# A fused short convolution and two-layer GELU network: which blocks use seven products instead of eight, with new instruction lists for four engines

## The chip, the cores and the metric

The kernel runs on one core of a Trainium2 chip. A core has TensorE (PE in the profile, with its weight loads as PEld), VectorE (DVE), ScalarE (ACT), GpSimd (POOL) and SyncE (SP), which run separate instruction queues and wait for one another by semaphores, and 16 DMA engines that serve transfers issued by SyncE, ScalarE and GpSimd. The metric is the device time of one execution in microseconds, less is better.

## The reference

```python
# x: 8 x 4096 x 192 (batch, sequence, features), 8 heads of 24 features, 7 taps
w = softmax(weight)                                   # 8 x 7, per head
out = sum over k of w[head, k] * x_padded[:, s + k]   # causal, zeros before the sequence
h = out.reshape(32768, 192) @ w_in                    # 192 x 2048
g = 0.5 * h * (1 + erf(h / sqrt(2)))                  # exact GELU
return g @ w_out                                      # 2048 x 192, float32
```

## The kernel before, in words

The 32768 tokens lie in two halves of 16384 that are worked on together, the one on partitions 0 to 63, the other on 64 to 127 (64 of the 192 features at a time). The tokens of each half are cut into 35 blocks (`NB`): blocks 0 to 5 have 256 tokens, blocks 6 to 34 have 512. What follows is about the blocks of 512.

For a block n, VectorE transposes the input (`t` n, line 1023) and adds up the seven taps of the convolution in float32 (line 359; the steps `1` to `6` of its lists); the zeroth tap is ScalarE's (`f0.n` to `f2.n`, line 1157). The sixth step writes `xc`, of which there are five buffers (`NXC`). TensorE multiplies `xc` by `w_in` (`mm1`, line 1292, 192 matmuls a block on quarter tiles of 64 x 64, four of which run side by side: 48 rounds); ScalarE applies GELU (line 1199, 16 instructions a block) and writes `gT` in bf16, of which there are two buffers. While TensorE is in block n with `mm1`, it also multiplies `gT` of block n-1 by `w_out`, in portions between the portions of `mm1`. There are two ways of doing this:

- In a plain block (`mm2_t`, line 1377) that is 192 matmuls, 48 rounds. Three transposes of VectorE (`ev.0`, `ev.1`, `ev.2`, line 477) bring the result from PSUM to the output buffer `osb`.
- In a seven-product block (those in `ST`; `mm2_s`, line 1426) some of the two-by-two products are formed the way Strassen and Winograd do, with seven products where eight stood: 44 rounds. This takes sums of parts of `gT`: `S1` (line 734, three parts), `S3` (737; parts 0 and 1 by accumulating DMAs of GpSimd, line 691, part 2 by VectorE), `Dn` (740, two parts) and `S4` (743, two parts). Behind the products come copies from PSUM by ScalarE (`p15`, `e`, `u`, `p3`, line 782), DMAs of GpSimd that copy `u` to the other partitions (`cu`, `cg`, line 686), combinations by VectorE (`k0`, line 790; `k3`, 797; `k4`, 803) and three transposes (line 815). Part 0 of `Dn` is VectorE's if the block before is a seven-product block too; otherwise it is made by two DMAs of GpSimd (`cp`, line 717, and `Dn.0`, line 721).

PSUM gives 2 x 2 banks to `mm1` (`hp`) and four to the second multiplication (`ob`); which of the four a block may use is worked out in advance (`BK`, `REL`), and TensorE waits for the step that frees a bank: `ev.2`, `k4`, `u`, `p3` or `e` of a seven-product block, the `ev` of a plain one.

The order on each engine is written out by hand. `LIST[n]` holds VectorE's steps while it prepares block n, as in `t19 ev.0.14 1 S1.0.16 2 ...` (name, part, block). `SLOT[n]` holds ScalarE's steps ahead of the i-th GELU of block n (`5:f2.20`). `GLIST` is GpSimd's order, with the copies of the last six tokens to the next block (`halo.n`, line 931). `AHEAD[n]` says up to which block SyncE has loaded before it stores block n-1 (`store`, line 845; four DMAs, one for each quarter of the partitions). The steps `w.0` to `w.9` make sums of the weights `w_out`, `evac` (line 438) brings the result of block 5 to `osb`. Block 34 ends the kernel: its products (line 1482) on whole tiles, four groups g of 128 tokens with two halves h, then `evac_half` (449 by VectorE, 451 by ScalarE) and `store_half` (459). The first group waits for the GELUs four by four:

```python
if (g, h) == (0, 0) and i % 4 == 0:
    t.wait_ge(S_GELU, SL0[m] + i + 4)
```

Of the kernel before, what the change touches and what calls it, by code (L numbers as in the profile page):

```python
# [11 lines left out]
def bass_lightweight_conv__then__act_gelu_exact_kernel(  # L12
# [41 lines left out]
    AHEAD = {4: 11, 5: 11, 7: 13, 8: 15, 9: 16, 10: 16, 11: 19, 12: 19, 13: 20, 14: 21, 15: 22, 16: 23, 17: 25, 18: 25, 19: 25, 22: 26, 23: 31, 24: 31, 25: 33, 26: 33, 27: 33, 28: 35, 29: 35}  # L54
# [20 lines left out]
    ST = [m for m in [8, 10, 11, 13, 14, 16, 17, 19, 20, 22, 24, 25, 27, 29, 30, 31, 32, 33] if m < M1]  # L75
    TYPE = {m: "S" if m in ST else "N" for m in range(-4, NB + 4)}
    LIST = {
        4: "t5 w.0.0 w.1.0 1 2 w.2.0 3 4 5 6",
        5: "t6 1 2 3 4 w.3.0 5 6",
        6: "w.4.0 t7 1 w.5.0 2 w.6.0 3 4 5 6",  # L80
        7: "t8 1 2 3 evac.0.5 w.7.0 4 5 6",
        8: "evac.1.5 t9 1 2 3 4 5 6",
        9: "ev.0.6 1 t10 2 ev.2.6 3 ev.1.6 4 5 w.8.0 6",
        10: "t11 1 2 S1.0.8 3 S1.1.8 ev.0.7 w.9.0 4 ev.1.7 S1.2.8 ev.2.7 Dn.1.8 S3.2.8 5 6",
        11: "S4.0.8 S4.1.8 k0.0.8 t12 1 2 3 ev.2.8 4 5 6",
        12: "t13 1 2 3 S1.0.10 4 ev.0.9 k4.0.8 k3.0.8 S1.1.10 5 ev.1.8 ev.0.8 ev.1.9 S1.2.10 S3.2.10 6",
        13: "Dn.1.10 S4.0.10 ev.2.9 1 S4.1.10 2 k0.0.10 3 4 S1.0.11 S1.1.11 Dn.0.11 ev.2.10 5 S1.2.11 Dn.1.11 S3.2.11 t14 6",
        14: "k4.0.10 t15 S4.0.11 S4.1.11 ev.0.10 k0.0.11 1 2 k3.0.10 3 ev.2.11 4 ev.1.10 5 6",
        15: "t16 1 2 S1.0.13 3 4 k3.0.11 ev.1.11 5 k4.0.11 S1.1.13 ev.0.12 ev.1.12 S1.2.13 ev.2.12 ev.0.11 Dn.1.13 S3.2.13 S4.0.13 S4.1.13 6",
        16: "t17 k0.0.13 1 S1.0.14 2 3 Dn.0.14 ev.2.13 S1.1.14 4 S1.2.14 S3.2.14 Dn.1.14 5 k4.0.13 ev.0.13 S4.0.14 S4.1.14 6",  # L90
        17: "k0.0.14 k3.0.13 t18 1 2 ev.2.14 3 4 ev.1.13 5 k4.0.14 6",
        18: "t19 ev.0.14 1 S1.0.16 2 ev.0.15 3 S1.1.16 4 k3.0.14 ev.1.15 ev.2.15 S1.2.16 ev.1.14 S3.2.16 Dn.1.16 5 S4.0.16 S4.1.16 6",
        19: "t20 k0.0.16 S1.0.17 1 2 ev.2.16 S1.1.17 3 4 S1.2.17 Dn.0.17 5 S3.2.17 k4.0.16 Dn.1.17 S4.0.17 S4.1.17 k0.0.17 k3.0.16 6",
        20: "1 t21 ev.2.17 ev.1.16 2 ev.0.16 3 4 5 6",
        21: "1 2 S1.0.19 t22 3 k4.0.17 ev.0.17 k3.0.17 ev.0.18 4 S1.1.19 S1.2.19 ev.1.18 S3.2.19 5 Dn.1.19 ev.2.18 6",
        22: "ev.1.17 S4.0.19 S4.1.19 k0.0.19 t23 1 S1.0.20 S1.1.20 ev.2.19 2 3 S1.2.20 4 S3.2.20 Dn.0.20 Dn.1.20 k4.0.19 S4.0.20 S4.1.20 k0.0.20 5 6",
        23: "1 t24 ev.2.20 k3.0.19 ev.0.19 ev.1.19 2 3 4 5 6",
        24: "S1.0.22 1 k3.0.20 ev.1.20 k4.0.20 ev.0.21 S1.1.22 t25 ev.0.20 2 ev.2.21 S1.2.22 ev.1.21 S4.0.22 Dn.1.22 S3.2.22 3 S4.1.22 4 k0.0.22 5 6",
        25: "t26 1 ev.2.22 2 3 4 5 6",
        26: "1 2 k4.0.22 t27 ev.0.23 3 ev.0.22 S1.0.24 4 S1.1.24 5 ev.1.23 S1.2.24 Dn.1.24 S3.2.24 k3.0.22 ev.2.23 ev.1.22 6",  # L100
        27: "S4.0.24 S4.1.24 k0.0.24 1 2 S1.0.25 Dn.0.25 S1.1.25 ev.2.24 3 4 S1.2.25 S3.2.25 t28 5 k4.0.24 Dn.1.25 S4.0.25 S4.1.25 k0.0.25 k3.0.24 6",
        28: "1 t29 2 ev.2.25 3 ev.0.24 ev.1.24 4 5 6",
        29: "1 2 S1.0.27 t30 3 S1.1.27 4 ev.0.26 k4.0.25 ev.1.26 S1.2.27 5 ev.2.26 k3.0.25 S3.2.27 ev.0.25 6",
        30: "ev.1.25 Dn.1.27 S4.0.27 S4.1.27 k0.0.27 t31 1 2 3 ev.2.27 4 5 6",
        31: "t32 1 k4.0.27 2 S1.0.29 3 4 5 ev.0.28 S1.1.29 k3.0.27 6",
        32: "S1.2.29 ev.2.28 ev.1.28 ev.1.27 S3.2.29 S4.0.29 ev.0.27 Dn.1.29 1 S4.1.29 k0.0.29 2 S1.0.30 3 t33 S1.1.30 ev.2.29 4 Dn.0.30 S1.2.30 S3.2.30 S4.0.30 5 Dn.1.30 k4.0.29 S4.1.30 k3.0.29 ev.1.29 k0.0.30 ev.0.29 6",
        33: "t34 S1.0.31 S1.1.31 1 ev.2.30 2 S1.2.31 Dn.0.31 Dn.1.31 S3.2.31 S4.0.31 S4.1.31 k4.0.30 3 4 k3.0.30 k0.0.31 5 6",
        34: "S1.0.32 S1.1.32 Dn.0.32 ev.2.31 1 ev.1.30 S1.2.32 S4.0.32 S3.2.32 ev.0.30 Dn.1.32 k4.0.31 2 S4.1.32 3 k0.0.32 4 5 S1.0.33 6",
        35: "ev.2.32 S1.1.33 S1.2.33 k3.0.31 Dn.0.33 ev.0.31 S4.0.33 S3.2.33 ev.1.31 k4.0.32 ev.0.32 k3.0.32 ev.1.32 Dn.1.33 S4.1.33 k0.0.33 ev.2.33 k4.0.33 ev.0.33 k3.0.33 ev.1.33",
# [3 lines left out]
        3: "0:f0.5 4:f1.5 5:f2.5 7:f0.6",  # L113
        4: "2:f1.6 5:f2.6 6:f0.7",
        5: "2:f1.7 6:f2.7",
        7: "0:f0.8 3:f1.8 3:f2.8 8:f0.9 9:f1.9 12:f2.9",
        8: "1:f0.10 5:f1.10 6:f2.10 10:f0.11 10:f1.11",
        9: "5:f2.11 7:p15.8 11:f0.12 14:e.8 15:f1.12",
        10: "0:u.8 2:p3.8 3:f2.12 5:f0.13 9:f1.13",
        11: "4:f2.13 6:p15.10 13:e.10",  # L120
        12: "0:p3.10 2:u.10 5:f0.14 6:p15.11 8:f1.14 9:f2.14 12:f0.15 13:e.11 15:f1.15",
        13: "0:u.11 2:p3.11 3:f2.15 7:f0.16 9:f1.16",
        14: "4:f2.16 6:p15.13 8:f0.17 11:f1.17 13:e.13",
        15: "0:p3.13 2:u.13 6:p15.14 10:f2.17 13:e.14 14:f0.18",
        16: "0:u.14 2:p3.14 4:f1.18 5:f2.18 9:f0.19 13:f1.19",
        17: "4:f2.19 6:p15.16 10:f0.20 10:f1.20 13:e.16",
        18: "0:p3.16 2:u.16 5:f2.20 6:p15.17 13:e.17 14:f0.21",
        19: "0:p3.17 3:f1.21 3:u.17 5:f2.21",
        20: "3:f0.22 6:p15.19 8:f1.22 10:f2.22 11:f0.23 13:e.19",
        21: "0:p3.19 2:u.19 6:p15.20 10:f1.23 10:f2.23 14:e.20 15:f0.24",  # L130
        22: "1:u.20 2:f1.24 3:p3.20 5:f2.24",
        23: "3:f0.25 6:p15.22 8:f1.25 11:f2.25 13:e.22 14:f0.26",
        24: "0:f1.26 2:u.22 3:p3.22 4:f2.26 12:f0.27",
        25: "0:f1.27 3:f2.27 6:p15.24 13:e.24",
        26: "0:p3.24 2:u.24 4:f0.28 6:p15.25 10:f1.28 10:f2.28 14:e.25 15:f0.29",
        27: "1:p3.25 3:u.25 5:f1.29 6:f2.29 12:f0.30",
        28: "1:f1.30 5:f2.30 7:p15.27 11:f0.31 13:e.27 14:f1.31",
        29: "0:u.27 1:f2.31 4:p3.27 7:f0.32",
        30: "1:f1.32 3:f2.32 7:p15.29 13:e.29",
        31: "0:p3.29 2:u.29 4:f0.33 6:p15.30 10:f1.33 10:f2.33 13:e.30 14:f0.34",  # L140
        32: "0:p3.30 2:u.30 6:p15.31 10:f1.34 10:f2.34 13:e.31",
        33: "0:p3.31 2:u.31 7:p15.32 14:e.32",
        34: "0:p3.32 2:u.32 7:p15.33 13:e.33 15:u.33",
        35: "0:p3.33",
# [50 lines left out]
    def sem(name):  # L195
        return es.enter_context(nc.semaphore(name))
# [4 lines left out]
    with es:  # L201
# [39 lines left out]
        S_OUT = [sem("S_OUT%d" % i) for i in range(2)]  # L241
        S_MSET = sem("S_MSET")
# [586 lines left out]
        def store(e, m):  # L829
# [13 lines left out]
            for q in range(4):  # L843

                e.dma_start(
                    ap(
                        outt,
                        ((q // 2) * HALF + OFF[m]) * C + (q % 2) * (C // 2),
                        [[C, 32], [32 * C, WS[m] // 32], [1, C // 2]],
                    ),  # L850
                    ap(
                        osb[m % 2],
                        32 * q * 8 * C,
                        [[8 * C, 32], [C // 2, WS[m] // 32], [1, C // 2]],
                    ),
                ).then_inc(S_OUT[m % 2], 16)

        GLIST = (
            "halo.10 cp.0.8 halo.11 S3.0.8 S3.1.8 Dn.0.8 cu.0.8 halo.12 halo.13 "
            "cg.0.8 cp.0.10 S3.0.10 Dn.0.10 S3.1.10 S3.0.11 S3.1.11 cg.0.10 cu.0.10 "  # L860
            "halo.14 halo.15 cg.0.11 cu.0.11 halo.16 cp.0.13 Dn.0.13 S3.0.13 S3.1.13 "
            "S3.0.14 S3.1.14 halo.17 cg.0.13 cu.0.13 cg.0.14 halo.18 halo.19 cp.0.16 "
            "cu.0.14 S3.0.16 Dn.0.16 S3.1.16 S3.0.17 S3.1.17 cg.0.16 cu.0.16 halo.20 "
            "halo.21 cp.0.19 cu.0.17 halo.22 cg.0.17 S3.0.19 Dn.0.19 S3.1.19 S3.0.20 "
            "S3.1.20 cg.0.19 halo.23 cu.0.19 cu.0.20 cp.0.22 halo.24 cg.0.20 S3.0.22 "
            "Dn.0.22 S3.1.22 halo.25 halo.26 cu.0.22 cg.0.22 cp.0.24 halo.27 S3.0.24 "
            "S3.1.24 Dn.0.24 S3.0.25 S3.1.25 cg.0.24 cu.0.24 halo.28 cg.0.25 halo.29 "
# [7 lines left out]
        def _(g):  # L875
# [89 lines left out]
            for op in GLIST.split():  # L965
                name, *q = op.split(".")
                if name == "halo":
                    halo(int(q[0]))
                else:
                    st_dma(g, int(q[1]), name, int(q[0]))  # L970
# [574 lines left out]
```

## Time and profile before

| | |
|---|---|
| median of 3 runs | 667.27 us (666.69 to 668.64) |
| the profiled execution | 665.89 us, its span 664.2 us |
| granted clock of TensorE | 1.00 |
| TensorE, VectorE, ScalarE, GpSimd busy | 658.3, 619.1, 598.3, 106.7 us |
| HBM read, written | 31.51 MB, 25.17 MB |
| GELU, line 1199 | 510 instructions of 1022 ns |
| taps, line 359, 128 x 1536 float32 | 145 instructions of 1805 ns |

Times in the profile count from the start of the span. Busy time is the time in which an engine executes an instruction; for TensorE it says little, since matmuls are pipelined and several run at once. A group of the profile is a line, an engine, an operation, the tiles and the number, then busy time, mean ns and the idle time of the engine just before, with what ended it.

### The profile page before, as it was taken

How to read it: one execution, taken by the hardware profiler on the slowest of the kernel's cores; microseconds unless marked ns; L12 is line 12 of the kernel's file. 1: busy time of each engine (PE TensorE's matmuls, PEld its weight loads, DVE VectorE, ACT ScalarE, POOL GpSimd, SP SyncE). 2: the span in 40 equal slices, each digit the busy share in tenths (PEclk: the TensorE clock that was granted, in tenths of full speed). 3: DMA queues.
4: the chain of work that ended last, by engine and by line, in shares of the span. 5: the costliest groups of instructions: out<-in, count | busy, mean ns of one | idle time of the engine just before them, and what ended most of it. 6: DMA issues, size and time to landing. Idle time of an engine off the chain costs nothing.

```text
span 664.2 us, 27974 instructions
## 1 busy us (share of the span) xinstructions
PE 658.3 (99%) x12792; PEld 505.6 (76%) x12792; DVE 619.1 (93%) x555; ACT 598.3 (90%) x707; POOL 106.7 (16%) x175
## 2 busy tenths in 40 slices
PE   8999999999999999999999999999999999999998
PEld 8999655576778988777878755767777888777887
DVE  6999879999999999999999999999999999999962
ACT  8899999898899899999989998988998988899883
POOL 7000430102010110202120102011212020111110
PEclk9999999999999999999999999999999999999999
DMA  9749493935673691677444348947545855352364
GB/s 156 163 95 181 74 156 82 218 64 116 150 146 80 141 206 25 164 168 150 94 116 114 65 106 207 200 108 168 113 106 120 177 117 126 66 113 49 86 142 112
DMA packets 146438, 83.66 MB, mean 126 GB/s; under 512 B 129936, under 2 KB 138192, under 8 KB 146320
## 3 DMA queue, kind: packets, MB, share of 16 engines
q1 hardware_dynamic: 129328, 49.42, 34.8%
q0 software_dynamic: 15872, 31.86, 23.7%
q8 instruction: 100, 1.64, 1.1%
q10 hardware_dynamic: 1120, 0.59, 0.3%
q14 instruction: 18, 0.15, 0.1%
HBM read 31.51 MB, written 25.17 MB: 85 GB/s over the span
## 4 chain that ended last, share of the span: by engine, by line
PE 96%; DMA 2%; ACT 1%; DVE 0%; issue 0%; POOL 0%; ACTq 0%; DVEq 0%
PE hp L1292 49%; PE ob L1426 25%; PE ob L1377 16%; PE ob L1332 5%; DMA win<-in_moe_w_in_dram 1%; PE hp L1482 1%; PE ob L1482 1%; DMA p5s<-u 1%; ACT gT L1199 0%; DMA wsb<-in_weight_dram 0%; DVE wcol L996 0%; POOL win L381 0%; DVE p5s L803 0%; POOL win L878 0%; POOL dg L901 0%
## 5 line engine op out<-in xcount | busy, mean ns | idle before, releaser
L1199 ACT ACTIVATE gT<-hp 128x1024 bf16<-128x1024 f32 x510 | 513.3, 1022 | 52.4 <-PE hp L1292 44.8
L1292 PE MATMUL hp<-xc,win 64*64 64x512 bf16 (+2 forms) x6036 | 438.6, 366 | 0.6 <-DVE win L381 0.5
L1292 PEld LDWEIGHTS hp<-xc,win 64*64 64x64 bf16 (+1 forms) x6036 | 241.8, 105 | 75.9 <-ACT gT L1199 7.3
L359 DVE SCALAR_TENSOR_TENSOR acc<-xT,wcol,acc 128x1536 f32<-128x1536 f32 (+1 forms) x165 | 282.0, 1709 | 8.3 <-ACT acc L1157 5.4
L1426 PE MATMUL ob<-gT,wot 64*64 64x512 bf16 x1152 | 219.1, 376 | 0.0
L1426 PE MATMUL ob<-gT,wst 64*64 64x512 bf16 (+2 forms) x1152 | 203.4, 323 | 0.5 <-DVE p5s L803 0.5
L1377 PE MATMUL ob<-gT,wot 64*64 64x512 bf16 x1920 | 135.8, 376 | 0.0
L1426 PE MATMUL ob<-s_S,wot 64*64 64x512 bf16 (+2 forms) x864 | 132.7, 305 | 0.0
L1426 PEld LDWEIGHTS ob<-gT,wst 64*64 64x64 bf16 x1152 | 98.8, 107 | 15.8 <-DVE p5s L803 1.3
L1377 PEld LDWEIGHTS ob<-gT,wot 64*64 64x64 bf16 x1920 | 71.0, 107 | 32.6
L1426 PEld LDWEIGHTS ob<-gT,wot 64*64 64x64 bf16 x1152 | 88.9, 107 | 8.6
L1426 PE MATMUL ob<-s_S,wst 64*64 64x512 bf16 x288 | 79.5, 376 | 0.0
L1426 PEld LDWEIGHTS ob<-s_S,wot 64*64 64x64 bf16 x864 | 68.8, 107 | 11.0 <-issue 0.3
L1157 ACT ACTIVATE acc<-xT,wcol 128x512 f32<-128x512 f32 (+1 forms) x93 | 64.6, 702 | 0.0
L1023 DVE STREAM_TRANSPOSE xT<-xin 128x1536 f32<-128x1536 f32 (+2 forms) x39 | 59.6, 1536 | 2.9 <-DMA xin<-in_x_dram 1.7
L691 POOL DMA_DIRECT2D gT<-gT x36 | 32.0, 907 | 186.3 <-DVE s_S L734 186.3
L1426 PE MATMUL ob<-s_Dn,wst 64*64 64x512 bf16 x216 | 61.0, 376 | 0.0
L359 DVE SCALAR_TENSOR_TENSOR xc<-xT,wcol,acc 128x1536 bf16<-128x1536 f32 (+1 forms) x33 | 56.5, 1713 | 0.6
L734 DVE TENSOR_TENSOR s_S<-gT 128x1024 bf16<-128x1024 bf16 (+1 forms) x54 | 45.7, 853 | 1.6 <-ACT gT L1199 1.6
L1332 PE MATMUL ob<-wout,gT 64*128 64x192 bf16 x768 | 42.0, 243 | 0.0
L1332 PEld LDWEIGHTS ob<-wout,gT 64*128 64x128 bf16 x768 | 35.1, 94 | 3.3
L1426 PEld LDWEIGHTS ob<-s_S,wst 64*64 64x64 bf16 x288 | 30.8, 107 | 4.4
(100 smaller groups left out, 423.6 us busy)
## 6 DMA issues: line engine op xcount, KB each, us to landing
out_dram<-osb SPq DMA_DIRECT2D x124, 192.0 KB, 3.4
xin<-in_x_dram SPq DMA_DIRECT2D x116, 192.0 KB, 4.5
gT<-gT POOLq DMA_DIRECT2D x18, 512.0 KB, 4.9
gT<-gT POOLq DMA_DIRECT2D x18, 256.0 KB, 4.6
dn<-gT POOLq DMA_DIRECT2D x6, 512.0 KB, 3.0
dn<-s_S POOLq DMA_DIRECT2D x6, 512.0 KB, 6.2
xin<-in_x_dram SPq DMA_DIRECT2D x18, 96.0 KB, 2.4
win<-in_moe_w_in_dram POOLq DMA_DIRECT2D x24, 64.0 KB, 3.3
```

What stands on the lines that cost most here:

```text
L359: return e.scalar_tensor_tensor(dst, src, wk, a, op0=ALU.mult, op1=ALU.add)
L691: e.dma_start(quad(m, 1, 0, k, k1 - k), quad(m, 0, 0, k, k1 - k), accum_op=ALU.add).then_inc(S_AD["S3.%d" % q], 16)
L734: ins = v.tensor_tensor(t("S1"), quad(m, 1, 0, k, n), quad(m, 1, 1, k, n), ALU.add)
L1023: v.transpose(out, src).then_inc(S_TR)
L1157: a.activation(out=acc[n % 2][:, p * TB : p * TB + w], in_=ap(xT[n % 2], p * XW + HX, [[NP * XW, 128], [1, w]]), func=AF.Copy, scale=wcol[ ...
L1199: a.activation(out=ap(gT[n % 2], (i % 2 * NF + i // 2) * TB if n in ST else i * c * 2 * w, dst), in_=ap(ob, 2 * TB, [[4 * TB, 128], *src[1 ...
L1292: ins = t.matmul(hbuf(u, slice(fo, fo + fw), o, w), ap(win, f1, [[NP * F, 64], [2, fw]]), xc[n % NXC][r, p * TB : p * TB + w], start=(p == ...
L1332: ins = t.matmul(bb[sub], gT[m % 2][r, c0 : c0 + 128], wout[r, CH[sub][i] * C : (CH[sub][i] + 1) * C], start=(ph == 0 and k == 0), stop=(p ...
L1377: ins = t.matmul(bank(BK[m][j], slice(64 * h, 64 * h + 64), w), ap(wot, 64 * hf * NF * C + CH[h][i] * C + 64 * j, [[NF * C, 64], [1, 64]]) ...
L1426: ins = t.matmul(bank(BK[m][bk], slice(64 * cg, 64 * cg + 64))[:, c0 : c0 + w], wt_, x, start=(e == mine[0]), stop=(e == mine[-1] or e in ...
L1482: ins = t.matmul(banks(m, g)[h], gT[m % 2][:, c0 : c0 + 128], wout[:, CH[h][i] * C : (CH[h][i] + 1) * C], start=(i == 0), stop=(i == NF - 1),)
```

## The change

Nineteen blocks instead of eighteen use seven products, and from block 8 on they come as pairs with a plain block between, until 29 to 33, which all do as before. What a seven-product block computes and transfers is unchanged. `LIST`, `SLOT`, `GLIST` and `AHEAD` are new throughout; three rows of each of the long ones are shown.

```diff
-    AHEAD = {4: 11, 5: 11, 7: 13, 8: 15, 9: 16, 10: 16, 11: 19, ..., 22: 26, 23: 31, ...}
+    AHEAD = {4: 12, 5: 13, 6: 14, 7: 14, 8: 14, 9: 16, 10: 17, 11: 17, ..., 22: 31, 23: 31, ...}
-    ST = [m for m in [8, 10, 11, 13, 14, 16, 17, 19, 20, 22, 24, 25, 27, 29, 30, 31, 32, 33] if m < M1]
+    ST = [m for m in [8, 9, 11, 12, 14, 15, 17, 18, 20, 21, 23, 24, 26, 27, 29, 30, 31, 32, 33] if m < M1]
     LIST = {
-        4: "t5 w.0.0 w.1.0 1 2 w.2.0 3 4 5 6",
+        4: "1 t5 2 3 4 5 6",
...
-        7: "t8 1 2 3 evac.0.5 w.7.0 4 5 6",
-        8: "evac.1.5 t9 1 2 3 4 5 6",
+        7: "t8 1 2 3 4 5 w.0.0 w.1.0 w.2.0 w.3.0 evac.0.5 w.4.0 w.5.0 6",
+        8: "w.6.0 evac.1.5 w.7.0 t9 1 2 3 4 5 w.8.0 6",
...
     SLOT = {
-        5: "2:f1.7 6:f2.7",
-        7: "0:f0.8 3:f1.8 3:f2.8 8:f0.9 9:f1.9 12:f2.9",
+        5: "1:f1.7 2:f2.7 6:f0.8",
+        7: "0:f1.8 2:f2.8 6:f0.9 9:f1.9 12:f2.9",
...
+        22: "0:p3.20 2:u.20 4:f0.24 6:p15.21 8:f1.24 9:f2.24 12:f0.25 13:e.21 15:f1.25",
...
-        34: "0:p3.32 2:u.32 7:p15.33 13:e.33 15:u.33",
-        35: "0:p3.33",
+        34: "0:p3.32 2:u.32 7:p15.33 14:e.33",
+        35: "0:u.33 0:p3.33",
...
     GLIST = (
-            "cu.0.31 S3.0.33 S3.1.33 cg.0.32 cu.0.32 cg.0.33 cu.0.33 "
+            "S3.1.32 cg.0.31 S3.0.33 S3.1.33 cg.0.32 cu.0.32 cu.0.31 cu.0.33 cg.0.33 "
```

The last rows of VectorE's list become

```
35 before: ... Dn.1.33 S4.1.33 k0.0.33 ev.2.33 k4.0.33 ev.0.33 k3.0.33 ev.1.33
35 changed: ... k0.0.33 k3.0.32 ev.1.32 ev.2.33 k3.0.33 k4.0.33 ev.1.33 ev.0.33
```

The store of block 33 is split: two quarters stay with SyncE, two go to the end of GpSimd's queue, with a semaphore of their own. In block 34 the first group's products take the first twelve of sixteen weight pieces for both halves before the last four of each.

```diff
-        def store(e, m):
+        def store(e, m, parts=range(4)):
...
-            for q in range(4):
+            for q in parts:
...
-                ).then_inc(S_OUT[m % 2], 16)
+                ).then_inc(S_OG if parts[0] else S_OUT[m % 2], 16)
...
+            store(g, NB - 2, (2, 3))
...
-                for h in range(2):
-                    for i in range(NF):
-                        if (g, h) == (0, 0) and i % 4 == 0:
-                            t.wait_ge(S_GELU, SL0[m] + i + 4)
+                cut = (0, NF - 4, NF) if g == 0 else (0, NF)
+                for i0, i1 in zip(cut, cut[1:]):
+                    for h in range(2):
+                        for i in range(i0, i1):
+                            if (g, h) == (0, 0) and i % 4 == 0:
+                                t.wait_ge(S_GELU, SL0[m] + i + 4)
...
-                store(sp, n - 1)
+                store(sp, n - 1, range(4) if n < NB - 1 else (0, 1))
...
+            sp.wait_ge(S_OG, 32)
```

## The prediction

> **What bounds the kernel now.** I read the page first (busy shares, chain), then busy times by stretch, then the waits of VectorE, then the timelines around the few stalls.
>
> ```profile
> PE 658.3 (99%) x12792; PEld 505.6 (76%) x12792; DVE 619.1 (93%) x555; ACT 598.3 (90%) x707; POOL 106.7 (16%) x175
> ...
> PE 96%; DMA 2%; ACT 1%; DVE 0%; issue 0%; POOL 0%; ACTq 0%; DVEq 0%
> ```
>
> The chain is TensorE from end to end. By stretch (columns: us, PE, PEld, DVE, ACT, POOL, clock, DMA share, GB/s):
>
> ```profile
> 86.00:630.00 544.00, 543.50 (x10603) 403.43 (x10599) 528.89 (x442) 497.76 (x577) 77.91 (x116) 1.00 0.59 125
> 630.00:664.20 34.20, 30.88 (x532) 26.13 (x524) 16.68 (x25) 20.77 (x27) 3.03 (x5) 1.00 0.53 129
> ```
>
> In the 544 us between block 7 and block 34, TensorE never rests and VectorE is busy for 529: TensorE bounds, VectorE has 15 us of idle time, of which some 5 are gaps of hundredths between instructions. The one visible stall of TensorE there (chain of waits):
>
> ```profile
> 572.87 0.48 ACT u L782
> 573.64 3.65 DMA p5s<-u
> 577.38 0.70 DVE p5s L803
> 578.12 0.85 PE ob L1426 x12
> ```
>
> The copy `cg` of block 29 lands late, `k4` of block 29 frees its bank late, and TensorE loses 0.66 us in block 31.
>
> **TensorE's saving.** From the first weight load of L1292 of one block to that of the next, the nine blocks 8 to 29 that multiply for a plain block take 20.69 us in the mean, the seventeen that multiply for a seven-product block 19.93 without that stall. Lists of 96 and 92 rounds at 0.216 us say 0.86, the means 0.76; one more such block: **-0.8 us**.
>
> **VectorE's added work.** Blocks 9, 12, 15, 18, 21, 23, 26 become seven-product, 10, 13, 16, 19, 22, 25 plain. The lists of both kernels differ by one S1 (three parts), one S3.2, three Dn, two S4, one k0, k3 and k4. Back to back, starts lie closer than durations: in the timeline 1.13 + 2 x 0.60 for S1, 0.60 S3.2, 1.15 Dn, 1.16 S4, 0.73 k0, 0.63 k4, 0.70 k3. Sum 1.13 + 1.20 + 0.60 + 3.45 + 2.32 + 2.06 = 10.75 us. Against it, a tap straight behind a tap of its block starts after 1.84, before anything else after 1.73; 61 such pairs become 41: -2.2. Small rest, each list summed by kind: **+8.9 us** up to the last tap of block 34.
>
> Is there room? Before, that tap ended at 629.3 and TensorE began block 34 at 629.7. VectorE had waited 8.4 us from list 4 to the taps of block 8 and 8.1 from there on:
>
> ```profile
> 83.64 0.56 DVE L438 COPY osb<-ob 128x384 f32<-128x384 f32 x1 [1.23 <-PE ob L1332]
> 89.39 1.82 DVE L359 SCALAR_TENSOR_TENSOR acc<-xT,wcol,acc 128x1536 f32<-128x1536 f32 x1 [3.51 <-ACT acc L1157]
> ```
>
> ```profile
> DVE acc L359 <- ACT acc L1157: 4.6, 3, 3.5
> DVE s_S L734 <- ACT gT L1199: 1.4, 3, 1.1
> DVE osb L477 <- PE ob L1377: 1.4, 2, 0.9
> DVE p5s L803 <- DMA p5s<-u: 1.0, 1, 1.0
> ```
>
> The new lists put the weight sums `w.0` to `w.6` where it idled (the first at 75.4; `w.2` is needed in block 7 at 84, `w.9`, done at 120, in block 9 at 125). `evac.1.5` still can't start before 83.64 (TensorE's products of block 5); behind it now `w.7`, `t9` and block 8's taps wait 3.1 us, and the first tap, with `f2.8` in slot 2 of block 7 instead of 3, starts at about 87.7 instead of 89.4. From there the old lists hold 530.0 us of work to the last tap of block 34, the new ones 537.6. So: 87.7 + 537.6 + 1.8 = 627.1 plus new waits, against a block 34 that could begin at 629.7 - 0.8 - 0.66 = 628.2. Room for 1.1 us of waits where there were 8.1.
>
> I walked both lists with no waiting step sooner than the trace shows its input after the block's start (eighth, twelfth, last Gelu of a block +10.8, +16.2, +21.0 us, or +11.3, +16.8, +21.7 beside plain products; k0 +10.4; ev.2 +17.65; k4 2.7 us after `u`). For the old lists this gives waits within 0.3 us of the 8.1; for the new, 1.1 (ev.1.7 waits 0.29 for block 7's products at 125.0, S1.2.8 0.15 for block 8's last Gelu at 104.1 + 21.7, S1.1.14 0.22, k4.0.30 0.33 for its copy, three others 0.1): VectorE is later in its lists, so most inputs are there. Its lead on TensorE, from a block's last tap to the block's start:
>
> | block | 11 | 18 | 24 | 29 | 31 | 33 | 34 |
> |---|---|---|---|---|---|---|---|
> | before, us | 15.6 | 9.5 | 5.2 | 12.2 | 18.6 | 3.1 | 0.4 |
> | changed, walked | 6.5 | 13.4 | 13.8 | 8.5 | 10.3 | 4.0 | 0.1 to 0.8 |
>
> So TensorE should not wait for taps, but block 34 has nothing to spare. In the same walk banks come free less than 0.4 us ahead of need in eleven places (`ev` or `k4` before blocks 10, 13, 15, 18, 19, 21, 22, 24, 25 and 33), before in seven, of which one was missed, by 0.66. A copy that lands late is now not made up, since no wait is left to absorb it. Old stall gone, **-0.66**; new ones **+0.8** (one as large as the old, and a little at block 34), ends 0 (all fits) and 7.0 (the 8.1 us stay, less the room of 1.1).
>
> **ScalarE.** `f0.8` goes from block 7 to block 5: 0.60 us more (its spacing) where the timeline shows gaps of 0.45 us up to block 7. Block 22 gets five taps beside four copies, as block 12 had, which took 20.11 us, 0.2 over the mean. Together **+0.2**, ends 0 and 0.8. The four added copies (1.8 us) hide: three blocks hold 48 Gelus at 0.96, nine taps at 0.60 and eight copies, 55 us in TensorE's 60.5. Without that cover they cost themselves.
>
> **The tail.**
>
> ```profile
> 649.97 1.16 PE L1482 MATMUL ob<-wout,gT 128*128 128x192 bf16 x12
> 651.64 0.59 PE L1482 MATMUL ob<-wout,gT 128*128 128x192 bf16 x5 [0.51 <-ACT gT L1199]
> ```
>
> TensorE rests 0.7 us until the last Gelu. In the new order 24 products at 0.0825 us come first, to 651.95, and the Gelu, with `u.33` now behind it, ends near 650.9: TensorE ends 0.68 earlier. But `u.33` is 0.75 later, `cu` stands ahead of `cg`, and ev.0.33 ends near 657.3 (ev.1.33: 656.4), with SyncE's and GpSimd's stores waiting behind. SyncE then has two stores fewer ahead of the half stores; GpSimd issues its two at 657.5 and 658.6.
>
> ```profile
> out_dram<-osb SPq DMA_DIRECT2D x124, 192.0 KB, 3.4
> xin<-in_x_dram SPq DMA_DIRECT2D x18, 96.0 KB, 2.4
> xin<-in_x_dram POOLq DMA_DIRECT2D x4, 96.0 KB, 4.1
> ```
>
> No row has such a store from GpSimd. Landing after 3.4 us (SyncE's) leaves the whole 0.68; after 5.1 (1.7 more, as for the loads) it lands at 663.7, near the old 663.8. Between them: **-0.4**, ends -0.7 and +0.2. The Trainium skill (DMA: Bandwidth & Descriptors, Specifications) gives the first byte as 1 us from GpSimd and 0.6 from SyncE; by that the stores land 0.4 later only and the tail term is -0.7. The rows say 1.7, at a crowded start.
>
> GpSimd's order is new too: S3, Dn and halo copies reach their readers with margins like the old ones, and loads come far ahead (SyncE's store of block 25 waits most, 9 us, with its buffer needed later). Nothing.
>
> **Sum.** -0.8 - 0.66 + 0.8 + 0.2 - 0.4 = -0.9: the profiled execution's 665.89 us (span 664.2) becomes 665.0; the median of the runs, 667.27, lies 1.4 above that execution and becomes **666.4 us**. About 0.3%, 2.0 us, is what a measurement of this kernel can tell from no change; this is less.
>
> **Rivals.**
> - All fits: no stall, whole tail, no ScalarE delay: -0.8 - 0.66 - 0.7 = -2.2, 665.1. For it: the walk closes with 0.1 us over. Against: one of seven tight spots was missed before, and there are eleven. 0.20.
> - VectorE late at block 34: its copies, sums and taps wait as they did. If most of the 8.1 us stay, TensorE stands for 4.2 us or more before block 34, or in bits earlier: 665.1 + 4.2 is where slower begins, all 8.1 give 672.1, half-way is 670.7. It decides from 5.3 us of waits in lists 9 to 34. For it: nothing absorbs a late DMA. Against: the waits were mostly VectorE being early. 0.23.
> - VectorE as plain bound: its idle time stays, and the 8.9 us come on top of the old time less the 0.4 us of lead: 675.8. The Trainium skill (Perfetto Trace Analysis, Identifying the Most-Contended Engine) calls matmul busy time a bad measure and would look at VectorE's 93%, which speaks against adding work there; here the chain's 96% speaks for TensorE. 0.05.
> - GpSimd's stores end last, small stalls besides: 667.3. 0.10.
> - The forecast: 0.42; its own range 665.3 to 668.2.
>
> That there is no nineteenth block is excluded: the instruction lists hold 304 Gelus written for it instead of 288.
>
> Faster by over 0.3% (below 665.27): most of the first rival and little of the forecast, 0.21. Slower (above 669.27): most of the second, all of the third, 0.27. Within: 0.52. The range from 664.8 to 671.0 leaves out the worst of VectorE's lateness and little below.
>
> **What would show it.** Right: TensorE's chain as before; blocks 10, 13, 16, 19, 22, 24, 27 at 19.9; VectorE's long waits between 90 and 630 under 2 us; the last tap of block 34 within 1 us of the first weight load of block 34; stalls of TensorE under 1 us in all. Wrong: rows with TensorE waiting for VectorE (osb, acc, s_S) of several us, above all ahead of block 34, or an end set by GpSimd's stores.

## The result: 0.5% slower, and the profile after

The changed kernel takes 669.83 us (median of 20 runs, 668.27 to 672.44), the kernel before 666.76 us (20 runs beside them, 665.78 to 668.64): ratio 1.0047, 95% interval 1.0038 to 1.0056. That is slower by more than the 0.3% that can be told from no change. Forecast were 666.4 and no visible change. The profiled execution took 669.30 us with a span of 667.6, against 665.89 and 664.2: +3.4 in both.

The page after, busy times and the chain's shares:

```profile
PE 659.0 (99%) x12808; PEld 486.1 (73%) x12808; DVE 626.6 (94%) x567; ACT 598.9 (90%) x711; POOL 112.5 (17%) x179
...
PE 94%; DVE 2%; DMA 1%; POOL 1%; issue 0%; ACT 0%; DVEq 0%; POOLq 0%
```

TensorE still carries the chain; VectorE has 7.5 us more to do. The stretch from block 7 to block 34 and the last 6.6 us (columns as in the prediction: stretch, us, PE, PEld, DVE, ACT, POOL, clock, DMA share, GB/s):

```profile
86.00:630.00 544.00, 543.96 (x10632) 386.15 (x10628) 537.47 (x456) 498.53 (x581) 79.66 (x117) 1.00 0.57 124
661.00:667.60 6.60, 0.00 (x0) 0.00 (x0) 0.00 (x0) 0.00 (x0) 0.00 (x0) 0.74 0.23 72
```

From 86 to 630 VectorE is busy for 537.5 of 544 us, and TensorE's matmuls still cover 543.96 of them. From 661 on no engine computes. The chain of waits ends there too. Its last pieces (start, us, what), after:

```profile
655.14 2.80 PE ob L1486 x32
657.95 2.65 PE hp L1486 x32
660.60 0.02 issue
660.62 0.33 ACT osb L452
```

The last piece before:

```profile
661.42 0.33 ACT osb L451
```

Counted from the end of this last copy of the output, the span went on for 2.4 us before. Now the copy begins 0.8 sooner and the span goes on for 6.6 us. From TensorE's last weight load for `mm1` to the end, the two traces show 15.14 us before and 18.88 after, so +3.74; that load itself begins at 649.02 before and 648.68 after, so -0.34. The sum, +3.4, is the whole change of the span. What comes ahead of the tail brought a little, the tail lost it tenfold.

What fills the tail is in SyncE's waits (line, released by: total us, times, longest), after:

```profile
SPq L201 <- PEq L201: 3.7, 1, 3.7
SPq L201 <- DMA out_dram<-osb: 1.3, 1, 1.3
```

Line 201 opens the `with` block in which the whole program stands, and what closes the program is put down to it. SyncE has seen the last store that it waits for land at 663.7, and then stands 3.7 us more (before: 0.2) at the end, where all engines meet. Which engine comes late is told by the rows of line 201, with durations in ns (min/median/max) and the first and last start, before:

```profile
L201 POOLq DRAIN  x1: 7748/7748/7748, 652.2 to 652.2; - x1
...
L201 SPq DRAIN  x1: 7/7/7, 663.9 to 663.9; - x1
```

and after:

```profile
L201 POOLq DRAIN  x1: 10334/10334/10334, 657.0 to 657.0; - x1
...
L201 ACTq DRAIN  x1: 153/153/153, 661.4 to 661.4; - x1
...
L201 SPq DRAIN  x1: 7/7/7, 663.9 to 663.9; - x1
L201 SPq EVENT_SEMAPHORE  x1: 17/17/17, 667.5 to 667.5; - x1
```

Every engine closes with a DRAIN, an instruction of its queue that isn't counted as busy. ScalarE's takes 0.15 us, SyncE's 0.007, GpSimd's 7.7 us before and 10.3 after. Before, it ran from 652.2 to 659.9 and was hidden, since SyncE came at 663.9. GpSimd's last transfer was then issued at 652.2 and landed at 654.9, 5.0 us ahead of the DRAIN's end (tiles written and read, issuing queue, count, KB each, us from issue to landing):

```profile
u<-u POOLq DMA_DIRECT2D x1, 128.0 KB, 2.7
```

After, the DRAIN stands behind the two quarter stores, the second of which lands at 662.3; it runs from 657.0 to 667.3, again 5.0 us beyond the landing, and the closing semaphore comes at 667.5. SyncE's own part ends at 663.9 in both kernels. (The wait's releaser in SyncE's row is named PEq, but TensorE's DRAIN, 1.7 us from 659.0, was long over: where several are waited for, the rows of the line itself tell which came last.)

### The profile page after: what moved, and what is told of

Same layout as the page of the kernel before. It is cut to its first block, busy times and chain, and to the rows that moved or that the text cites. A ratio compares the mean times of both kernels' runs of the same rounds, so it can differ in the third digit from the quotient of the medians.

```text
span 667.6 us, 28045 instructions
## 1 busy us (share of the span) xinstructions
PE 659.0 (99%) x12808; PEld 486.1 (73%) x12808; DVE 626.6 (94%) x567; ACT 598.9 (90%) x711; POOL 112.5 (17%) x179
## 4 chain that ended last, share of the span: by engine, by line
PE 94%; DVE 2%; DMA 1%; POOL 1%; issue 0%; ACT 0%; DVEq 0%; POOLq 0%
PE hp L1294 48%; PE ob L1428 26%; PE ob L1379 14%; PE ob L1334 4%; PE ob L1486 1%; PE hp L1486 1%; DVE acc L360 1%; DMA xin<-in_x_dram 1%; DMA win<-in_moe_w_in_dram 1%; DVE xT L1025 1%; POOL win L879 0%; POOL xTb L375 0%; DVE xc L360 0%; ACT gT L1201 0%; DVE acc L354 0%
## 5 line engine op out<-in xcount | busy, mean ns | idle before, releaser
L1294 PE MATMUL hp<-xc,win 64*64 64x512 bf16 (+2 forms) x6036 | 433.3, 366 | 0.3 <-DVE xc L360 0.2
L1294 PEld LDWEIGHTS hp<-xc,win 64*64 64x64 bf16 (+1 forms) x6036 | 231.1, 105 | 84.4 <-ACT gT L1201 8.2
L1428 PE MATMUL ob<-gT,wst 64*64 64x512 bf16 (+2 forms) x1216 | 213.8, 323 | 0.0
L1428 PE MATMUL ob<-s_S,wot 64*64 64x384 bf16 (+2 forms) x912 | 138.4, 305 | 0.0
L1428 PEld LDWEIGHTS ob<-gT,wst 64*64 64x64 bf16 x1216 | 103.2, 107 | 19.0 <-DVE gsm L804 1.7
L1428 PEld LDWEIGHTS ob<-gT,wot 64*64 64x64 bf16 x1216 | 94.3, 107 | 7.1 <-DVE osb L816 0.4
L1428 PE MATMUL ob<-s_S,wst 64*64 64x512 bf16 x304 | 83.9, 376 | 0.0
L1428 PEld LDWEIGHTS ob<-s_S,wot 64*64 64x64 bf16 x912 | 72.5, 107 | 15.7
L1379 PEld LDWEIGHTS ob<-gT,wot 64*64 64x64 bf16 x1728 | 58.5, 107 | 34.7
L1428 PE MATMUL ob<-s_Dn,wst 64*64 64x512 bf16 x232 | 65.5, 376 | 0.0
L932 POOL COPY xT<-xT 128x18 f32<-128x18 f32 x29 | 21.3, 735 | 105.2 <-DVE xc L360 93.2
```

The costliest lines, as they stand in the source:

```text
L932: g.tensor_copy(dst, src).then_inc(S_HALO)
L1294: ins = t.matmul(hbuf(u, slice(fo, fo + fw), o, w), ap(win, f1, [[NP * F, 64], [2, fw]]), xc[n % NXC][r, p * TB : p * TB + w], start=(p == ...
L1379: ins = t.matmul(bank(BK[m][j], slice(64 * h, 64 * h + 64), w), ap(wot, 64 * hf * NF * C + CH[h][i] * C + 64 * j, [[NF * C, 64], [1, 64]]) ...
L1428: ins = t.matmul(bank(BK[m][bk], slice(64 * cg, 64 * cg + 64))[:, c0 : c0 + w], wt_, x, start=(e == mine[0]), stop=(e == mine[-1] or e in ...
```

## The experiments

Two readings were to be told apart: that the two stores on GpSimd's queue set the end (through the DRAIN behind them), or that the new lists, the order of block 34's products or crowded stores do. Then: what the DRAIN's end goes by. "Before" stands for runs of the kernel before on the same chip.

**e1: the changed kernel with block 33's whole store on SyncE.**

```diff
-            store(g, NB - 2, (2, 3))
...
-                store(sp, n - 1, range(4) if n < NB - 1 else (0, 1))
+                store(sp, n - 1)
...
```

> The changed kernel with all four quarters of block 33's store back on SyncE, nothing else changed. Theory A (GpSimd's closing drain sets the end: it ran from 657.0 to 667.4 us in the changed kernel, while SyncE had seen every store landed at 663.7): the end falls to about 664.0 in the span, 3.6 less, so about 666.2 us and 0.1% below the kernel before; GpSimd's drain ends before 661. Theory B (VectorE's and TensorE's lists cost the 3 us, the drain only happens to stand last): it stays at 669 or more.

Measured: 665.17 us (12 runs) beside 666.26 before, ratio 0.9983 [0.9973, 0.9992]; profiled 665.17, span 663.4. Line 201 in e1:

```profile
L201 POOLq DRAIN  x1: 7588/7588/7588, 651.6 to 651.6; - x1
...
L201 SPq DRAIN  x1: 7/7/7, 663.2 to 663.2; - x1
```

GpSimd is through at 659.2, and SyncE ends the program at 663.2. The loss is gone and a gain of 1.1 us is left, itself under the 0.3% named above: the store's place is the whole loss.

**e2: the kernel before, with only the store split** as in the change (old lists, old order of products).

```diff
...
+            store(g, NB - 2, (2, 3))
...
-                store(sp, n - 1)
+                store(sp, n - 1, range(4) if n < NB - 1 else (0, 1))
...
```

> The kernel before with the one part that puts two quarters of block 33's store at the end of GpSimd's queue; lists, block types and products as before. Theory A: GpSimd's last transfers land near 662.7 instead of 654.9, its drain ends about 5 us behind them, near 667.7, and the time rises by 3 to 4 us to about 670. Theory B: nothing over 0.5 us.

Measured: 669.85 us (6 runs), 1.0055 [1.0039, 1.0071]; profiled 669.29, span 667.6. Line 201 in e2, and GpSimd's two stores among the transfers of its last 24 us:

```profile
L201 POOLq DRAIN  x1: 10104/10104/10104, 657.2 to 657.2; - x1
...
L201 SPq DRAIN  x1: 7/7/7, 664.0 to 664.0; - x1
```

```profile
out_dram<-osb POOLq DMA_DIRECT2D x2, 192.0 KB, 4.7
```

The loss is there without any of the lists. The two stores are the only thing that moved, the second landed at 662.4, and GpSimd's DRAIN ended at 667.3, 4.9 us later.

**e8: the changed kernel with one quarter on GpSimd instead of two.**

```diff
-            store(g, NB - 2, (2, 3))
+            store(g, NB - 2, (3,))
...
-                store(sp, n - 1, range(4) if n < NB - 1 else (0, 1))
+                store(sp, n - 1, range(4) if n < NB - 1 else (0, 1, 2))
...
```

> The changed kernel with one quarter of block 33's store on GpSimd instead of two. If the drain ends 5.0 us behind the landing of GpSimd's last transfer (before: landing 654.9, drain to 660.0; changed: 662.4 and 667.4), the landing comes some 0.7 to 1.2 us earlier and so does the end: 668.6 to 669.1 us. If the drain's length follows the number of runs that GpSimd writes (7.75 us before, 10.33 changed), it shrinks by more, toward 667.5.

Measured: 667.45 us (12 runs), 1.0017 [1.0006, 1.0028]; profiled 666.86, span 665.1. Line 201 and the transfers at the end of e8:

```profile
L201 POOLq DRAIN  x1: 8931/8931/8931, 655.9 to 655.9; - x1
```

```profile
out_dram<-osb POOLq DMA_DIRECT2D x1, 192.0 KB, 4.0
```

The one store is issued at 655.95 and lands 4.0 later, at 659.9; the DRAIN ends at 664.9. Half the transfer, a landing 2.4 us sooner, an end 2.5 us sooner: that is what an end 5.0 us behind the landing gives. But the landing came sooner than expected, and the time is the one that was expected if the DRAIN's length followed the amount that GpSimd writes, so e8 by itself doesn't tell the two apart. The other traces do. Before and e5 have the same transfers on GpSimd; the last lands 2.7 us after its issue in one and 2.2 in the other, and the DRAIN takes 7.75 and 7.21 us, so its end is 5.0 us behind the landing in both. And in e7 below, which has the transfers of e1, the DRAIN takes 6.2 us where it takes 7.6 in e1.

**e3: the changed kernel with the two quarters on ScalarE,** behind its store of the second group (g is 1).

```diff
-            store(g, NB - 2, (2, 3))
...
+                if g == 1:
+                    store(a, NB - 2, (2, 3))
```

> The changed kernel with the two quarters issued by ScalarE, behind its store of group 1, instead of GpSimd. Theory A: no transfer of GpSimd is late, so its drain ends before 661 and the time is that of the store on SyncE alone or up to 0.3 us less, about 666.0. If two late issues of any second engine cost the 3 us: 669 or more.

Measured: 665.00 us (12 runs) beside 665.99, 0.9986 [0.9975, 0.9998]; profiled 665.19, span 663.5. Taking the stores off SyncE is harmless when the other queue isn't GpSimd's; it isn't measurably better than SyncE alone (e1) either.

**e6 and e7: e1 with a late instruction on GpSimd** at the moment when it issued the stores. e6 copies 16 KB from one on-chip buffer to another, e7 fills the same 16 KB without a transfer. Both overwrite weights that nothing reads any more.

```diff
+            wait_ev(g, NB - 2, NP - 1)
+            g.dma_start(dg[:, 0:64], idb[:, :]).then_inc(S_OG, 16)     # e6
+            g.memset(dg[:, 0:64], 0.0).then_inc(S_OG)                  # e7 instead
...
```

> The store of block 33 on SyncE, and GpSimd ends with one small transfer within SBUF (128 rows of 128 bytes), issued when block 33's result is there, near 656.1. It writes weights that nothing reads any more. If the drain ends 5 us behind the landing of GpSimd's last transfer, that is near 658.5 + 5 = 663.5, level with the other engines: time as with the store on SyncE, within 0.3 us, and the drain in the trace ends at 663 to 664. If the drain takes 10 us after any late transfer: 667 in the span, about 669.3 us. If it follows the amount: ends before 661.

> The store of block 33 on SyncE, and GpSimd ends with a small fill of memory at the same moment instead of a transfer. If the drain is about transfers, it ends as with the store on SyncE alone, before 661, or with the fill at 656.5, and the time does not change. If any late work of GpSimd starts a long drain: 666 or later in the span.

Measured: e6 666.26 us (11 runs), 1.0001 [0.9991, 1.0011], profiled 666.69, span 665.0; e7 665.58 us (12 runs), 0.9993 [0.9982, 1.0003], span 664.4. GpSimd's last instruction in the timeline of e6 and its row of line 201:

```profile
657.10 0.57 POOL L973 DMA_DIRECT2D dg<-idb  x1 [4.25 <-DVE osb L450]
```

```profile
L201 POOLq DRAIN  x1: 7650/7650/7650, 657.1 to 657.1; - x1
```

and the same two of e7:

```profile
656.88 0.15 POOL L973 MEMSET dg<- 128x64 bf16 x1 [4.01 <-DVE osb L816]
```

```profile
L201 POOLq DRAIN  x1: 6223/6223/6223, 656.9 to 656.9; - x1
```

The small copy lands after 2.5 us (659.6) and the DRAIN ends at 664.7, 5.1 us later; it comes last, SyncE having come at 664.3. So neither the way to the output nor the size is what matters. The fill has nothing in flight (GpSimd's last transfer had landed at 654.8), and its DRAIN still takes 6.2 us, to 663.1. That is neither of the two outcomes expected: the DRAIN isn't about transfers alone. SyncE came later (664.2), so it cost nothing. These two executions also ran some 0.7 us later than e1 up to their tails, so of their total only the last microsecond is of use here. In time alone e6 can't be told from before; the reading rests on its rows.

**e10: e6 with the copy 3.6 us later,** behind block 34's last part on VectorE.

```diff
-            wait_ev(g, NB - 2, NP - 1)
+            wait_ev(g, NB - 1, 3)
```

> As the small transfer of GpSimd behind the store on SyncE, but issued 3.3 us later, when VectorE has brought out its last part of block 34 (about 660.4 after the same start). If the drain ends about 5 us behind the landing of GpSimd's last transfer, the span ends 5.0 + 2.5 us after the issue, near 668: 3 us more than with the early small transfer, about 669.3. If the drain only needs some fixed time from the end of GpSimd's lists, of 6 us as behind the fill: 666.7 in the span, about 668.3. If a transfer of 16 KB costs no more than its landing: 665.5 or less.

Measured: 669.96 us (6 runs) beside 666.34, 1.0058 [1.0040, 1.0076]; profiled 670.20, span 668.4. GpSimd's last instruction in the timeline of e10, its landing and line 201:

```profile
660.71 0.56 POOL L973 DMA_DIRECT2D dg<-idb  x1 [7.80 <-DVE osb L450]
```

```profile
dg<-idb POOLq DMA_DIRECT2D x1, 16.0 KB, 2.4
```

```profile
L201 POOLq DRAIN  x1: 7516/7516/7516, 660.7 to 660.7; - x1
```

Sixteen kilobytes that no one reads cost as much as the change's 384 KB. The copy lands at 663.1 and the DRAIN ends at 668.2, 5.1 us later, as in e6; a fixed time from the issue (6.2 us, which the fill alone would have allowed) would have ended it at 666.9. In e10 every store of the output is on the queue that it had before, so crowded stores aren't what the loss needs.

**e5: the kernel before with only the new order of block 34's products** (the `cut` loop).

> The kernel before with the new order of block 34's first products alone. By the prediction's term the 0.66 us in which TensorE waited for the last Gelu is filled with twelve more products: 0.5 to 0.7 us less, about 666.1. Rival: the end is set by the last store half and SyncE's queue, and nothing changes.

Measured: 665.99 us (12 runs), 1.0000 [0.9989, 1.0012]; span 664.1. The order does what it says: TensorE's first products start at 650.10 instead of 649.97 and its last group (line 1484) at 658.03 instead of 658.58, so 0.68 us are saved between. Nothing comes out of it, and SyncE's timeline (start, us, what) shows why, before and in e5:

```profile
656.47 2.60 SPq L845 DMA_DIRECT2D out_dram<-osb  x4
659.12 2.57 SPq L459 DMA_DIRECT2D out_dram<-osb  x4
```

```profile
656.83 2.34 SPq L845 DMA_DIRECT2D out_dram<-osb  x4
659.21 2.95 SPq L459 DMA_DIRECT2D out_dram<-osb  x4
```

SyncE issues the four stores of block 33 and, behind them, the four half stores of block 34, and is through with it at 661.7 before and 662.2 in e5. The last of them lands at 663.2 before and 663.8 in e5, ScalarE's last half store at 663.8 before and 663.4 in e5: ScalarE's comes sooner, SyncE's later. SyncE's half stores stand in a queue, not behind TensorE.

**e9: e5 with two of those four stores on ScalarE,** as in e3.

> The kernel before with the new order of block 34's products and two quarters of block 33's store on ScalarE. The new order alone ended TensorE at 660.8 instead of 661.4 and gave nothing, since SyncE's eight last issues then ran until 662.1. If SyncE's queue took the gain, it comes out here: 0.4 to 0.7 us less than before. If the order has nothing to give, or the tail is bound elsewhere: within 0.2 us of before.

Measured: 665.65 us (12 runs) beside 666.34, 0.9984 [0.9973, 0.9996]; profiled 665.73, span 664.0 (this execution came 0.8 us late to its tail, GpSimd's DRAIN starting at 653.0 instead of 652.2). SyncE in e9:

```profile
657.28 0.85 SPq L846 DMA_DIRECT2D out_dram<-osb  x2
658.17 3.25 SPq L460 DMA_DIRECT2D out_dram<-osb  x4
```

With the queue shortened, the half stores start 0.94 sooner than before and the old lists come to -0.7 us. From TensorE's first product of block 34 to SyncE's DRAIN the traces show 13.97 us before, 13.83 in e5 and 12.99 in e9. That supports SyncE's queue as what held e5's gain; it is one execution of each, and the intervals of e5 and e9 overlap, so it isn't shown beyond doubt.

**e4: the changed kernel with block 33's store on SyncE and the old order of products,** so the nineteen blocks and the lists alone.

```diff
...
-                cut = (0, NF - 4, NF) if g == 0 else (0, NF)
+                cut = (0, NF)
...
```

> The changed kernel with the store of block 33 on SyncE and the old order of block 34's products: only the lists and the block types differ from the kernel before. In the changed trace the last Gelu ended at 650.35, before the first twelve products would have, at 650.63, since u.33 now stands behind it; so the order should matter by 0.0 to 0.2 us: 666.2 to 666.4. By the prediction's term it would cost 0.68.

Measured: 665.36 us (12 runs) beside 665.99, 0.9988 [0.9978, 0.9998]: the lists are worth 0.6 us. The profiled execution, 664.43, was a quick one of these. Here too TensorE stands nowhere in the first group: its products start at 648.70 and the second group's at 651.35, which is 32 products back to back, since the last Gelu, with `u.33` moved behind it, ends at 649.41 and so ahead of the first twelve products. Beside the new lists the new order of products has nothing left to fill.

Four versions beat both kernels, e1, e3, e4 and e9, the kernel before by 0.12 to 0.17%. Their intervals leave out 1, but this is under the 0.3% named above, and they can't be told from one another. The one nearest to the change is e1: the change, with GpSimd's two stores given back to SyncE.

## Why the prediction was wrong

**The step that failed is the tail's term,** forecast as -0.4 us with ends -0.7 and +0.2; from the last `mm1` weight load to the end it measured +3.74. Its first half held in its amount: TensorE no longer rests in the first group, and the last output copy begins 0.80 us sooner, 0.34 of it from the blocks ahead and 0.46 from the first group; a pause of 0.2 ahead of the third group, which began at 655.14, took the rest of the 0.68. The step behind it was only half right: as e4 shows, moving `u.33` behind the last Gelu brings this alone, and the new order of products, which the working counted on, adds nothing to it. But SyncE's side didn't follow: it was through at 663.9 in both kernels. Beside GpSimd's stores its four half stores took 4.0 us to land in the median, where they took 2.4 before and 2.4 in e1, and ScalarE's last half store, the last landing that SyncE waits for, was issued 0.8 sooner but took 2.7 us instead of 2.0 and landed at 663.7 as before. Without any DRAIN the tail would have been 0.3 longer, just beyond the forecast's end of +0.2.

The second half weighed one cost of a store on GpSimd, when the data land: issues at 657.5 and 658.6, landing by 663.7 at worst. That was even too careful: they were issued from 656.5, took 4.7 us each, and the second landed at 662.3. The working put what GpSimd does after its last transfer at nothing, without a reason. The row was in the trace of before, 7748 ns at line 201, and neither the page's busy times nor the chain of waits contains it, since it isn't counted as work. With the 5.0 us behind the landing that the trace of before already showed (the last copy for block 33 landed at 654.9, the DRAIN ended at 659.9), the forecast's own landings, 662.0 to 663.7, give an end at 667.0 to 668.7; the span was 667.6. e2 shows that this one step explains the loss without the rest of the change, e1 that the rest has none.

**The rival with GpSimd's stores ending last** had the right place and the wrong price: 667.3 took the landing as the end and had no DRAIN in it. It had a chance of 0.10, and an end set by GpSimd's stores was named among the signs of being wrong. The rival that gave 670.7, VectorE late at block 34, comes near the time by accident; its mechanism is absent, as follows. That the measured 669.83 lies within 664.8 to 671.0 is luck too: the range reached so far up for VectorE's lateness.

**TensorE's saving held.** Blocks 10, 13, 16, 19, 22 and 24, 27, which were to show 19.9 us, show 20.02, 19.89, 19.90, 20.13, 19.88, 19.82 and 19.87 between their first weight loads; block 10 had 20.74 before.

**The walk of VectorE's lists held.** VectorE's longer waits from 90 to 630 us, after:

```profile
DVE osb L478 <- PE ob L1379: 0.8, 1, 0.8
DVE s_S L735 <- PE ob L1428: 0.2, 1, 0.2
DVE p5s L804 <- DMA p5s<-u: 0.2, 1, 0.2
```

Counted like for like, VectorE's pauses of over 0.12 us come to 1.45 us, before to 6.5; those of over 0.08 us to 2.5, before to 8.0. Forecast were 1.1 beside 8.1. The first of the rows is `ev.1.7`, the last `k4.0.30`, both named ahead. The first tap of block 8 started at 87.81 (forecast 87.7), the lead at block 34 was 0.46 us (0.1 to 0.8), and the leads at blocks 11, 18, 24, 29, 31 and 33 were 6.3, 13.2, 13.6, 8.0, 9.9 and 3.3, each within 0.7 of the walk. The added work was sized at 8.9 us up to block 34's last tap, and busy time, which counts otherwise, rose by 7.5.

**The stalls held.** In the profiled execution TensorE stands for some 0.7 us in all in blocks 10, 19, 25, 31, 33 and 34, no more than 0.2 at once: forecast +0.8, but in small pieces instead of one large one, and the old stall of 0.66 is gone. Other executions of the same lists do have a large one: block 10, 20.02 us here, took 20.50 in e1 and 20.76 in e3, there behind a copy that landed late. ScalarE's term of +0.2 was needless: block 22, where it was expected, is among the quick ones. In its place a load of `w_out` landed late in the first blocks and cost 0.29. e8 and e10 show such a wait too, the other traces don't; whether the new lists have a part in it isn't shown.

So the lists' terms, -0.8 - 0.66 + 0.8 + 0.2 = -0.46, stand against -0.34 in the trace, or -0.63 without that late load, and against -0.6 us in e4, which has what the moved `u.33` brings in the first group besides. The whole forecast was -0.9; e1, the change without its GpSimd stores, gives -1.1. The Trainium skill's rule of the most contended engine (Perfetto Trace Analysis, Identifying the Most-Contended Engine), which points at the engine of highest occupancy, VectorE with 93%, stood behind the rival with VectorE as plain bound and its chance of 0.05. The trace speaks against that rival: VectorE took its added work at 94% and no wait of TensorE for taps appeared.

**The sentence on the first byte** (the Trainium skill, DMA: Bandwidth & Descriptors, Specifications: 0.4 us between GpSimd and SyncE) asked for a tail of -0.7. In the changed kernel's tail SyncE's two quarter stores took 2.8 us from issue to landing and GpSimd's two 4.7: 1.9 apart, near the 1.7 of the loads that the forecast had taken. But this was not the term that mattered.

## What to carry to other kernels

Read the rows of the program's end before moving anything there: here GpSimd's closing DRAIN runs for some 5 us behind the landing of its last transfer, and it is free only as long as the other engines end later than that. A transfer late on GpSimd's queue is thus priced at its landing plus 5 us, whatever its size (16 to 192 KB here), and given to another queue if that reaches past the end. Behind a late instruction without a transfer the DRAIN still took 6.2 us (e7, a single trace). The chain of waits doesn't show this; compare the chain's last piece with the end of the span (2.4 us before, 6.6 after).

## What the runs showed of the hardware

- GpSimd's DRAIN ended 4.9 to 5.1 us after the landing of GpSimd's last transfer in all eleven traces in which it stands directly behind one (5.0 before and after, 4.9 in e2, 5.1 in e1, 5.0 in e8, 5.1 in e6 and e10), while its length went from 7.2 to 10.3 us; the transfers had 16 to 192 KB, between on-chip buffers or to HBM. With no transfer in flight (e7) it ended 6.1 us after the fill. The other engines' took between 0.007 and 1.7 us. What the engine does in that time no row shows.
- A wait at the program's end was put down to TensorE's queue, which had been done 7 us before; the engine that came last was GpSimd.
